# Shifted value tiles of the first batch made by TensorE with a shifted identity in place of a second read from scratch, with a newly searched order

**The chip, the cores and the metric.** One core of one Trainium2 chip. The metric is the device time of one execution in microseconds (us); a lower time is better. Of several executions the median is quoted with the lowest and highest. The runs of this study fell on several chips, and the same kernel took about 230 us on one and about 239.5 us on two others; so kernels are compared only with the kernel before on the same chip, by their ratio.

## The reference

Block-sparse attention over 4 batches, 8 heads, 768 positions and 64 values a head, followed by a gated feed-forward layer. The mask lets a block of 32 queries see its neighbours, the first and the last block, and three random blocks.

```python
def _attn_ref(q, k, v, sampled_blocks):
    ...                                   # scores = q k^T / sqrt(64)
    mask = np.abs(blk_i - blk_j) <= 1     # window
    mask = mask | (blk_i == 0) | (blk_j == 0) | (blk_i == n_blocks - 1) | (blk_j == n_blocks - 1)
    ...                                   # plus three sampled blocks for each block of queries
    return softmax(scores where mask) @ v

def _moe_ref(x, w_in, g_ln, w_sg, b_sg, w_out):
    h = gelu(x @ w_in); u, v = halves of h
    v_s = einsum('ts,bsd->btd', w_sg, layer_norm(v) * g_ln) + b_sg
    return x + (u * v_s) @ w_out
```

## The kernel before

The kernel is one list of named operations. Each has an engine, the keys that it reads and writes, and a function that issues the instructions. Every engine runs its own operations strictly in the order of the list; the waits are derived from the keys.

```python
SEQ = """ ... regsP0 w_in0 ... ga0.3
vg0.0 kp0.5 ga0.5 ... va0.0 va0.1 ... vs0 ga0.4 vg0.1 ... vgc0 ... exG0.1 pvG0.0:4 pvW0.0 ga0.1 pvR0.0 ... """
```

V of a batch is written to a scratch area in memory and read back in several layouts.

```python
for n in range(2):
    def vg_(e, n=n):                                   # rows 0-31 and 736-767 of V
        return e.dma_start(vj[64 * n:64 * n + 64, 0, :, :].rearrange("p h e -> p (h e)"),
                           bass.AP(sc.tensor, sc.offset, [[736 * 520, 2], [520, 32], [1, 520]]))
    op("SP", f"vg{b}.{n}", vg_, r=[("scr", bp)], w=[("vjg", n)] + [("vjp", p_) for p_ in range(4)], ..., nbytes=66560)

def vgc(x): ...                                        # compact copy of both halves: VG
op(("DVE", "ACT"), f"vgc{b}", vgc, r=["VGz", ("vjg", 0), ("vjg", 1)] + ..., w=[("VG", n) for n in range(4)], ...)
op("SP", f"vs{b}", lambda e: e.dma_start(VS[...], sc[64:704, :]...), r=[("scr", bp)], w=["VS"], ..., nbytes=665600)
op("SP", f"va{b}.1", lambda e: e.dma_start(VA[:, 1:5, ...], sc[128:640, :]...), ..., nbytes=532480)
...                                                    # va.0 and va.5: the first and the last tile of VA
```

VA holds V in six tiles of 128 rows. VS holds the same rows 64 rows later. VG holds the rows of the first and last block, which every query sees. The attention of a group of queries is three kinds of product into one accumulator: `pvG` with VG, then `pvW` with VA and VS, then `pvR` with the gathered random blocks VR. So VG comes first.

The softmax here doesn't subtract the row's maximum and nothing guards it: scores larger than these inputs give would overflow.

## Time and profile before

| | kernel before |
|---|---|
| time, first three runs | 232.17 us median (229.5 to 235.98) |
| time on the chip of the first experiments | 230.41 us median (229.43 to 232.35, 7 runs) |
| span of the profile shown in the prediction | 240.6 us |
| span of a second profile, taken among the experiments | 227.6 us |

The profile that the prediction reads is of an execution of 242.57 us, well above the median, and so it is no fair partner for the changed kernel. The comparisons below use the second profile, of an execution of 229.72 us. The head of its page: the span, and the busy time of the engines (share of the span, instructions).

```profile
span 227.6 us, 8125 instructions
PE 199.9 (88%) x3282; PEld 159.9 (70%) x3282; DVE 157.1 (69%) x469; ACT 166.9 (73%) x254; POOL 110.3 (48%) x207
```

The busy times by stretches of the same profile (columns as the prediction explains them):

```profile
22.70:36.00 13.30, 7.40 (x228) 5.92 (x230) 5.50 (x27) 8.88 (x14) 11.75 (x26) 0.50 1.10 245
36.00:57.40 21.40, 18.08 (x458) 14.25 (x455) 12.35 (x42) 16.97 (x23) 11.78 (x20) 0.90 1.00 208
57.40:227.60 170.20, 166.42 (x2555) 134.77 (x2551) 130.68 (x370) 126.26 (x195) 77.51 (x139) 1.00 0.66 159
```

TensorE (the first pair) is idle for 5.9 + 3.3 us in the first two stretches. The timelines of SyncE's queue, VectorE and TensorE show the chain that the change attacks (start, duration, then the idle time before and what ended it):

```profile
20.40 0.70 SPq L572 DMA_DIRECT2D vj<-scr  x1
22.05 0.52 SPq L582 DMA_DIRECT2D VS<-scr  x1
25.10 0.55 SPq L572 DMA_DIRECT2D vj<-scr  x1
32.52 0.47 DVE L332 COPY VG<-vj 64x260 bf16<-64x260 bf16 x2 [3.70 <-DMA vj<-scr]
33.13 0.59 PE L335 MATMUL PS<-VG,PG 128*128 128x130 bf16 x4 [3.38 <-DVE VG L332]
```

The second half of VG is issued at 25.10 us, the copy runs at 32.52 us, and the first value product starts at 33.13 us after a wait of 3.38 us.

### The profile page before, as it was taken

To read this page: it belongs to the slowest core of one execution; us is meant where nothing else is said; L and a number is where in the kernel's file an instruction comes from. 1 tells how busy PE (TensorE), PEld (TensorE's weight loads), DVE (VectorE), ACT (ScalarE), POOL (GpSimd) and SP (SyncE) were. 2 spreads that over 40 slices of the span, in tenths; PEclk is the share of its full clock that TensorE was granted. 3 is DMA by queue.
4 is the path that set the end of the run, shared out by engine and by line. 5 is a ranking of instruction groups with operands and counts; after the bars stand their busy time and mean duration, and the time that the engine had idled before them with its cause. 6 is when DMAs were issued, how large, how long until landed. Compare 5 with 4: busy or idle time off the path is not lost.

```text
span 240.6 us, 8125 instructions
## 1 busy us (share of the span) xinstructions
PE 206.9 (86%) x3282; PEld 164.1 (68%) x3282; DVE 157.0 (65%) x469; ACT 166.9 (69%) x254; POOL 109.3 (45%) x207
## 2 busy tenths in 40 slices
PE   5064538879999989999699999799999999999994
PEld 2053426558887678887488687678886778789672
DVE  2453323645796978894648967648668957577694
ACT  3497926868698946898479666578999677976100
POOL 8215984544384856911547373803472752012000
PEclk9999999988999999999979999999999999999999
DMA  6999999759997795985977975690588123311007
GB/s 191 341 368 282 268 198 228 141 116 235 277 212 178 217 241 75 214 130 183 219 192 169 275 150 185 153 179 9 138 258 208 36 54 119 111 46 44 3 0 262
DMA packets 34457, 41.51 MB, mean 173 GB/s; under 512 B 4804, under 2 KB 27620, under 8 KB 34420
## 3 DMA queue, kind: packets, MB, share of 16 engines
q0 software_dynamic: 14208, 16.20, 35.7%
q1 hardware_dynamic: 20212, 24.80, 34.0%
q8 instruction: 26, 0.43, 0.7%
q14 instruction: 11, 0.09, 0.1%
HBM read 39.72 MB, written 9.55 MB: 205 GB/s over the span
## 4 chain that ended last, share of the span: by engine, by line
PE 78%; ACT 9%; DMA 3%; SPq 3%; issue 3%; another core or an unknown queue 2%; DVE 1%
PE PS L335 68%; PE PS L848 5%; PE PS L521 4%; DMA x_tok<-in_q_dram 3%; ACT PW L707 2%; SPq L480 2%; ACT PR L750 1%; ACT QD L331 1%; ACT PG L724 1%; PE PS L659 1%; ACT w_sgT L331 1%; ACT qn L331 1%; ACT L724 1%; ACT bsg L331 1%
## 5 line engine op out<-in xcount | busy, mean ns | idle before, releaser
L616 POOL DMA_INDIRECT VR<-scr,IDX x44 | 43.2, 982 | 20.5 <-issue 8.3
L637 POOL COPY KR<-KT 128x128 bf16 x88 | 26.0, 328 | 24.7 <-PE PS L335 19.9
L335 PE MATMUL PS<-w_sgT,vh 128*128 128x384 bf16 x192 | 33.5, 326 | 0.0
L633 DVE COPY KR<-KT 128x128 bf16 x176 | 28.3, 226 | 4.1 <-PE PS L335 3.2
L335 PE MATMUL PS<-w_in,xg 128*128 128x512 f32 x96 | 28.3, 422 | 3.1 <-ACT xg L331 2.2
L335 PE MATMUL PS<-w_out,xg 128*128 128x512 f32 x96 | 26.3, 409 | 0.0
L335 PE MATMUL PS<-xg,w_in 128*128 128x384 f32 x128 | 26.2, 351 | 0.0
L916 DVE SCALAR_TENSOR_TENSOR gt<-PS,gcol,bsg 128x384 f32<-128x384 f32 x32 | 19.3, 613 | 10.1 <-PE PS L335 9.3
L335 PEld LDWEIGHTS PS<-w_sgT,vh 128*128 128x128 bf16 x192 | 17.9, 98 | 11.0 <-issue 0.4
L750 ACT ACTIVATE PR<-PS 96x1024 bf16<-96x1024 f32 (+1 forms) x23 | 21.7, 962 | 5.0 <-PE PS L335 2.8
L335 PEld LDWEIGHTS PS<-xg,w_in 128*128 128x128 f32 x128 | 23.1, 194 | 1.7 <-ACT QD L331 0.3
L707 ACT ACTIVATE PW<-PS,b_odd 128x512 bf16<-128x512 f32 (+1 forms) x24 | 15.5, 652 | 9.2 <-PE PS L335 9.2
L335 PEld LDWEIGHTS PS<-w_in,xg 128*128 128x128 f32 x96 | 17.2, 194 | 6.9 <-ACT xg L331 2.7
L874 POOL TENSOR_TENSOR lnt<-lnmv,lnc 128x2 f32<-128x2 f32 x12 | 2.4, 200 | 42.5 <-DVE lnmv L870 41.8
L707 ACT ACTIVATE PW<-PS,b_even 128x512 bf16<-128x512 f32 (+1 forms) x24 | 15.6, 651 | 8.0 <-remote 4.4
L934 DVE TENSOR_TENSOR x_tok<-PS,x_tok 128x512 f32<-128x512 f32 x24 | 16.3, 685 | 5.7 <-PE PS L335 5.5
L869 DVE BATCH_NORM_STATS2 lnst<-vg 128x6 f32<-128x512 f32 x24 | 16.1, 682 | 5.6 <-ACT vg L867 5.6
L829 DVE RECIPROCAL rden<-PS 128x8 f32<-128x8 f32 x24 | 4.9, 205 | 22.7 <-PE PS L335 20.6
L335 PEld LDWEIGHTS PS<-w_out,xg 128*128 128x128 f32 x96 | 17.1, 189 | 3.3
L331 ACT ACTIVATE QD<-PS 64x768 bf16<-64x768 bf16 x18 | 14.4, 803 | 6.3 <-PE PS L335 4.5
L724 ACT ACTIVATE PG<-PS 128x512 bf16<-128x512 f32 x24 | 13.9, 598 | 6.4 <-PE PS L335 6.3
L335 PE MATMUL PS<-VA,PW 128*64 128x65 bf16 x384 | 17.5, 199 | 0.1
(122 smaller groups left out, 438.4 us busy)
## 6 DMA issues: line engine op xcount, KB each, us to landing
out_dram<-x_tok SPq DMA_DIRECT2D x20, 256.0 KB, 2.3
VR<-scr SPq DMA_DIRECT2D x114, 32.5 KB
scr<-vj SPq DMA_DIRECT2D x4, 780.0 KB, 4.7
VS<-scr SPq DMA_DIRECT2D x4, 650.0 KB
kn<-in_v_dram POOLq DMA_DIRECT2D x6, 384.0 KB
kn<-in_k_dram POOLq DMA_DIRECT2D x6, 384.0 KB
qn<-in_q_dram POOLq DMA_DIRECT2D x6, 384.0 KB, 7.3
VA<-scr SPq DMA_DIRECT2D x4, 520.0 KB
```

Source lines behind the costliest of these rows:

```text
L331: return x.activation(o_, i_, ACT.Copy)
L335: return pe.matmul(o, l, r, start=start, stop=True, skip_group_check=True)
L616: return g.indirect_dma_start(out=vt[0:96, :, :].rearrange("p h e -> p (h e)"), out_offset=None, in_=scr[bp][:, :], in_offset=bass.Indirec ...
L633: ins = x.tensor_copy(KR[:, :, rg, 32 * j:32 * j + 32], KT[:, :, bass.ds(vals["DVE", j, i], 32)])
L637: op("POOL", f"kp{b}.{i}", lambda x, i=i, rg=rg: x.tensor_copy(KR[:, :, rg, 64:96], KT[:, :, bass.ds(vals["POOL", 2, i], 32)]), r=kk + [(" ...
L707: return a.activation(o, i_, ACT.Exp, bias=bias[:, 0:1], scale=SCALE)
L724: op("ACT", f"exG{b}.{tau}", aft=ga, fn=lambda a: a.activation(PG[pg_][:, :], PS[:, uG.slot * 512:uG.slot * 512 + 512], ACT.Exp, scale=SCALE),
L750: return a.activation(PR[pr_][0:96, 0:n], PS[0:96, uR.slot * 512:uR.slot * 512 + n], ACT.Exp, scale=SCALE)
L848: ins = pe.transpose(PS[:, cc:cc + P], x_tok[bp][:, tau, kt * P:kt * P + P], ident_f[:, :])
L869: op("DVE", f"bs{b}.{tau}", lambda x: x.bn_stats(lnst[:, vr, :], vg[vr][:, :]), r=[("vg", vr)], w=[("lnst", vr)], dur=0.6, prio=pr - 300)
L916: op("DVE", f"g1{b}.{c}{dt}", lambda x: x.scalar_tensor_tensor(gt[gr][:, :], PS[:, u.slot * 512:u.slot * 512 + 384], gcol[:, dt:dt + 1], b ...
L934: op("DVE", f"res{b}.{tau}", lambda x: x.tensor_tensor(x_tok[bp][:, tau, :], PS[:, u.slot * 512:u.slot * 512 + 512], x_tok[bp][:, tau, :], ...
```

## The change

Its intent: in batch 0, where transfers bound the kernel, drop the 650 KB read of VS and let TensorE make the five tiles. A product of VA's tile with an identity that is shifted by 64 columns moves rows by 64 partitions; two such products into one accumulator give one tile of VS for half the heads. The shifted identity lives in the buffer of the later tile `bsg`, so the profile shows the shift products as `PS<-VA,bsg`. With it comes a wholly new list, found by a search in which landings were assumed late. One more line of the diff is not shown: an operation on GpSimd now also waits for a zeroing or padding operation (names in `ze` and `pa`) that stands just before it there.

```diff
+    op(("DVE", "POOL"), "i3z", lambda x: x.memset(I3, 0.0), w=["I3"], ...)
+    op("POOL", "i3", lambda g: g.affine_select(I3, I3, compare_op=ALU.not_equal, fill=1.0, base=64, ...), ...)
...
-        op("SP", f"vs{b}", ... VS <- sc[64:704] ..., w=["VS"], nbytes=665600)
+        if b == 0:
+            for t in range(5):
+                def shf(pe, t=t, u=u):
+                    for c in range(2):
+                        for n in range(2):
+                            ins = mm(pe, PS[:, o:o + 260], I3[:, 128 - 128 * c:256 - 128 * c],
+                                     VA[:, t + c, 4 * n:4 * n + 4, :]..., c == 0)
+                ...  op("PE", f"shf{t}", shf, r=["I3", ("VA", t), ("VA", t + 1)], ...)
+                     op(("DVE", "ACT"), f"she{t}", copy accumulator -> VS[:, t], ...)
+        else:
+            op("SP", f"vs{b}", ... as before, w=[("VS", t) for t in range(5)])
...
-SEQ = ... the old list ...
+SEQ = ... padv:P csq0.1 ... vg0.0 va0.1 csk0.3 ... qkG0.1:0 shf1:6 ga0.1 ... va0.0 shf3:2 ... shf0:0 ... she0 vg0.1 ... vgc0 pvG0.0:6 ...
+      ... gV1.5 bs1.5 ... vg2.0 vg2.1 ba1.5 ... qkQ2.1:0 vgc2:A gU1.02 nv1.3:A nv1.2:A nv1.4:A ...
```

## The prediction

> **What bounds the kernel now.** I read the page first, then the busy time of each engine by stretches, then TensorE's waits in the start, then who waited for the scratch reads, and last the issues of SyncE in order of time. The stretches were chosen by hand at the places where TensorE changes from waiting to working.
>
> Busy time in each stretch; the first pair of numbers is the stretch and its length, then busy time (instructions) of PE, PEld, DVE, ACT and POOL, the granted clock, the DMA share and the rate:
>
> ```profile
> 0.00:22.70 22.70, 8.88 (x55) 5.59 (x55) 8.46 (x33) 14.91 (x22) 9.47 (x24) 1.00 0.90 296
> 22.70:36.00 13.30, 6.97 (x204) 5.49 (x204) 4.75 (x24) 7.75 (x14) 11.74 (x26) 1.00 1.08 237
> 36.00:57.40 21.40, 17.66 (x423) 13.82 (x421) 10.21 (x40) 15.18 (x21) 11.46 (x20) 0.92 0.82 175
> 57.40:237.00 179.60, 172.97 (x2606) 139.23 (x2603) 133.13 (x373) 129.04 (x199) 76.61 (x139) 0.99 0.64 151
> ```
>
> From 57.4 to 237 us TensorE is busy 172.97 of 179.60 us (96%): that part is TensorE's own work, and the change touches it only through a new order. In the first 57.4 us TensorE idles 13.8 + 6.3 + 3.7 = 23.9 us, and there the DMA share is 0.8 to 1.1, that is, all 16 queues have work almost without a gap. So batch 0 is bound by transfers, batches 1 to 3 by TensorE.
>
> What TensorE waited for between 22 and 50 us (total, times, longest):
>
> ```profile
> PE PS L335 <- DVE VG L332: 2.9, 1, 2.9
> PE PS L335 <- ACT w_sgT L331: 2.6, 1, 2.6
> ...
> PE PS L335 <- ACT PW L707: 1.2, 1, 1.2
> PE PS L335 <- DVE KR L633: 1.1, 1, 1.1
> ```
>
> The largest is the first product with V (at 32.84 us), which waits for the compact tile VG. The reads behind VG, and who waited for them:
>
> ```profile
> L572 SPq DMA_DIRECT2D vj<-scr x8: 537/553/692, 20.3 to 177.6; - x8
> ...
>   DVE VG L332: 3.5, 1
> ```
>
> So VG in its turn waits for a read of scratch. SyncE's issues show why that read is late:
>
> ```profile
> 20.27 0.69 SPq L572 DMA_DIRECT2D vj<-scr  x1
> 21.02 0.38 SPq L580 DMA_DIRECT2D VA<-scr  x1
> 21.43 0.43 SPq L584 DMA_DIRECT2D VA<-scr  x1
> 21.91 0.52 SPq L582 DMA_DIRECT2D VS<-scr  x1
> 22.65 1.37 SPq L611 DMA_DIRECT2D VR<-scr  x3
> 24.90 0.56 SPq L572 DMA_DIRECT2D vj<-scr  x1
> ```
>
> The second half of VG (24.90) stands behind VA, behind the 650 KB of VS, and behind a gather. VectorE copies it at 32.3 us, some 7 us after its issue. VS is the shifted value tile: the same rows as VA, 64 rows later, read a second time.
>
> **What the Trainium skill says.** "DMA: Bandwidth & Descriptors", section Issuing engines are not separate DMA queues: transfers started by different engines run on the same 16 DMA engines and interleave. The trace agrees: the reads of scratch share 20 to 32 us with w_in and the gathers of GpSimd, at a share of 1.09. [...]"TensorE: Matmul & The Clock Gate", section Back-to-back issue gap, gives N/2.4 + 2.5 ns warm and N/1.2 ns cold, and section LDWEIGHTS columns/1.2. The trace agrees on loads (98 ns for 128 bf16 columns) and on two speeds: the 16 value products of a group start about 27 ns apart at 33.5 us and 17 ns apart at 47 us.
>
> **The change, part by part.** (1) Removed: one read of 650 KB, in batch 0 only, of 41.51 MB in all. Between vg's first half (20.27) and VG's copy (32.3) the SyncE queue moved about 65 + 98 + 520 + 650 + 98 + 65 KB = 1.5 MB in some 11.3 us, 0.13 MB/us, because it shares with GpSimd's queue. At that rate 650 KB are worth 0.65/0.13 = 5.0 us; at the whole stretch's 280 GB/s they are worth only 2.3 us. So VG, and the first value product with it, can come 2.3 to 5 us earlier: 28 to 30.5 us in place of 32.84.
>
> (2) Added on TensorE: 5 tiles of 4 products, 260 columns each. By the page's formula, an estimate, 111 ns warm or 217 ns cold each, beside loads of 98 ns: 0.45 to 0.9 us a tile, 2.2 to 4.4 us in all. Three of the five stand before the first value product, in idle TensorE time (6.3 us of it between 22.7 and 36). Two (shf2, shf4) stand among later work, where TensorE is 83% busy: about 1 us of real cost.
>
> (3) Added evictions: 128x520 from the accumulator to the tile. A like ACT eviction (PG, 128x512 to bf16) took 598 ns, a like DVE one (xg, 128x512) 679 ns; two on ACT and three on DVE give 1.2 + 2.1 = 3.3 us. Both engines are under 60% busy from 22.7 to 36 us. Only the one before the first value product (she0, 0.7 us) could be on the path, and it overlaps the wait for VG.
>
> (4) Added set-up: a memset and a select for the shifted identity, under 1 us (the like ones took 0.21 and 0.29 us), in GpSimd's idle 8.4 us of the start. Six warming products at the start go (2.7 us of TensorE, in its idle time).
>
> (5) The order. V is loaded first, so the write to scratch no longer waits for the tenth load. Before it was issued at 15.53 us and scratch could be read at 20.27. At one load per 1.06 us (landings at 13.58, 14.64 and 15.69), V's four loads among the first five land at about 10.3, the copies end near 12, and the write goes out there. It stands behind the q loads already queued, though, so I give it 1 us. One k load now follows the write: 4.7 + 0.8 MB still must pass before the first scores, which stay at about 22.5 us (22.77 before). w_in can start earlier on GpSimd, at 11 to 12 in place of 16.64 us, which takes bandwidth from q but returns it to V.
>
> (6) The rest of the list is a new search result with no other change in work. TensorE's idle time from 57.4 to 237 us is 6.6 us, and of it a new list may win or lose a couple.
>
> Sum: the first value product 3 to 5 us earlier, less 1 us of TensorE for two shifts, less what a later wait gives back. The next ones are gathers: the first gather product also has waits for instructions in it (0.50 and 0.52 us at 35 us), and ACT stood 4.4 us before 35.88 with a releaser that the profile doesn't know. If a third comes back, 2 us remain in the first stage; for the search with late landings I add 1.5 us. The profiled run took 242.57 us against a median of 232.17, so the profile shows more waiting than the timed runs have, which is why I keep to the lower end. 232.2 - 2.0 - 1.5 is 228.7, I say 228.5.
>
> **The rivals.** First, the read was hidden anyway: the gathers for the same group (SyncE's nine issues from 25.66 us, 5.1 us long) may end the wait instead. For: pvR0.0 comes directly after. Against: those gathers stand in the same queue behind VS and move forward with it. Time: 231 to 233. Second, a wait takes the place of the removed one: the shift products stand in TensorE's list ahead of the scores of the other tiles, so a late VA holds up scores that had not needed VA. For: VA is 520 KB and read after the later write. Against: it is now second in the queue. Time: 232 to 235. Third, the load order loses: a k load behind the scratch write and w_in earlier could move the first scores to 24 or 25 us. Time: about 231. Fourth, the searched order is robust: fewer late landings stop TensorE, so idle from 36 us on falls by half (5 us) as well. For: the three runs before spread from 229.5 to 235.98, as a kernel at the mercy of its landings would. Time: 223 to 226.
>
> **Range and chances.** The bounds: the work on TensorE after 22.7 us is 6.97 + 17.66 + 172.97 = 197.6 us; with 1 to 2 us of shifts, a start at 22.5, 3.6 us of tail and 2 us outside the span, the floor is about 227 in the profile's own speeds, somewhat less with a warmer clock. So gains beyond 9 us are nearly out; 223 is my lower end. Upper end 233.5, where a new wait eats all. Faster by over 2% means under 227.5: 0.40; within 2%: 0.52; slower: 0.08.
>
> **What would show it.** Right: no VS read in batch 0; the first product with VG at 28 to 30.5 us; TensorE's wait for VG below 1 us; 20 products with the shifted identity of 0.45 to 0.9 us a tile; TensorE idle of 22.7 to 57.4 us down from 10 to 6 or 7 us; first scores at 22 to 23.5 us. Wrong: a new long wait of TensorE for VA in front of shf1, first scores after 24 us, a first value product still after 32 us, or more TensorE idle after 57 us than 6.6 us. The number is wrong too if the new list changes batches 1 to 3 by more than 3 us, which I can't read from the list.

## The result and the profile after

The changed kernel took 239.72 us median (238.25 to 240.25, 4 runs) against 231.75 us (229.5 to 235.98, 4 runs): a ratio of 1.0367 with a 95% interval of 1.027 to 1.0464. It is slower by over 2%. A ratio here is the mean time of one kernel's fast runs over the mean of the other's fast runs of the same rounds, so it is not quite the ratio of the medians. Two further controls on two chips gave 1.0303 and 1.0323.

The head of the page of the changed kernel (execution of 238.25 us):

```profile
span 236.4 us, 8156 instructions
PE 203.8 (86%) x3296; PEld 164.2 (69%) x3296; DVE 159.7 (68%) x474; ACT 165.7 (70%) x252; POOL 110.8 (47%) x209
```

Of the 8.8 us between the spans (236.4 against 227.6) TensorE's busy time accounts for 203.8 - 199.9 = 3.9 us and its idle time for the other 4.9 us. The two profiles may be of different chips; the two controls below, on one chip, differ in span by 9.6 us (237.2 against 227.6). By stretches:

```profile
22.70:36.00 13.30, 9.23 (x207) 6.72 (x202) 6.01 (x31) 8.61 (x14) 10.52 (x24) 0.96 1.04 195
36.00:57.40 21.40, 17.99 (x454) 13.99 (x452) 11.14 (x46) 16.78 (x24) 12.11 (x23) 0.87 0.88 178
57.40:236.40 179.00, 170.28 (x2587) 138.01 (x2584) 132.32 (x368) 126.54 (x198) 74.89 (x138) 0.98 0.64 153
```

From 22.7 to 57.4 us TensorE's idle time is 4.1 + 3.4 = 7.5 us against 9.2 us before: it did fall. But after 57.4 us it is 8.7 us against 3.8 us. (The clock of 0.96 says little here: the trace's first clock record is at 31.54 us.) The list of TensorE's waits (total, times, longest), without the 11.9 us before its very first product:

```profile
...
PE PS L338 <- ACT vh L919: 4.6, 2, 4.2
PE PS L338 <- issue: 3.3, 3, 2.2
PE PS L338 <- DMA VA<-scr: 2.7, 1, 2.7
...
PE PS L338 <- DVE VG L335: 0.8, 1, 0.8
```

Three things stand here. The wait for VG fell from 3.4 to 0.8 us; a new wait for VA of 2.7 us stands in its place; and there is a wait of 4.2 us for `vh`, the gate's input, that the kernel before did not have. (The 2.2 us called `issue` are a pause inside the fourth tile's shift products, up to 40.61 us, for which the profile names no cause; the second profile has 1.84 us there.) The timelines of SyncE's queue and of TensorE in batch 0:

```profile
18.56 0.70 SPq L579 DMA_DIRECT2D vj<-scr  x1
24.06 0.56 SPq L579 DMA_DIRECT2D vj<-scr  x1
26.69 1.91 PE L338 MATMUL PS<-VA,bsg 128*128 128x260 bf16 x8 [2.71 <-DMA VA<-scr]
28.83 1.07 PE L338 MATMUL PS<-VA,bsg 128*128 128x260 bf16 x4
32.50 0.41 PE L338 MATMUL PS<-VG,PG 128*128 128x130 bf16 x4 [0.82 <-DVE VG L335]
```

The first half of VG is issued 1.8 us earlier than before (18.56 against 20.40), VS is gone, and still the first product with VG starts at 32.50 us, only 0.6 us earlier than before. The idle time in which it used to wait now holds twelve shift products (eight in 1.91 us and four in 1.07 us) and a wait for VA ahead of them. The first two tiles took 0.87 us each (from 26.69 us to the next product at 28.43 us).

The `vh` wait is found where batch 1's feed-forward layer meets batch 2's attention. SyncE's queue, ScalarE and TensorE between 110 and 130 us:

```profile
110.02 6.28 SPq L579 DMA_DIRECT2D vj<-scr  x2
121.36 0.85 ACT L334 ACTIVATE VG<-vj 64x260 bf16<-64x260 bf16 x2 [4.35 <-DMA vj<-scr]
125.03 4.02 PE L338 MATMUL PS<-w_sgT,vh 128*128 128x384 bf16 x12 [4.16 <-ACT vh L919]
```

The new list puts the compact copy of VG of batch 2 on ScalarE, ahead of three normalisations (`nv1.3`, `nv1.2`, `nv1.4`) that make `vh` for batch 1. The copy waits 4.35 us for the two halves, everything behind it on ScalarE waits with it, and TensorE stands 4.16 us. The chain that ended last shows why the read took so long (start, length):

```profile
110.02 5.76 DMA vj<-scr
115.79 5.54 DMA vj<-scr
```

The two halves do not overlap. Each has the keys `vjp` among its writes, so the second is ordered behind the landing of the first, although they write different rows. The same holds in batch 0: the issues are at 18.56 and 24.06 us in the timeline above, and the first half's last data landed at 24.04 us. In the prediction's list of issues, too, the second half follows the first by 4.6 us (24.90 us, and the first half landed at 24.89 us); I had read that as standing behind other reads.

The stall costs more than its 4.16 us. Busy times in the five microseconds after it, the changed kernel:

```profile
125.00:130.00 5.00, 4.97 (x29) 2.46 (x30) 2.70 (x7) 3.74 (x6) 0.64 (x1) 0.50 0.51 150
```

After the stall the granted clock is 0.50, and the twelve gate products take 4.02 us. Where no stall stands ahead of them, the same twelve take 2.12 us (a run below). The Trainium skill, "TensorE: Matmul & The Clock Gate", section What's actually happening, says that the array falls to half its clock after about 3.4 us of idleness and needs as long to come back; this trace agrees with the halving, after 4.16 us of waiting.

### The profile page after: what moved, and what is told of

The parts are those of the page before. It is cut to its first block, busy times and chain, and to the rows that moved or that the text cites.

```text
span 236.4 us, 8156 instructions
## 1 busy us (share of the span) xinstructions
PE 203.8 (86%) x3296; PEld 164.2 (69%) x3296; DVE 159.7 (68%) x474; ACT 165.7 (70%) x252; POOL 110.8 (47%) x209
## 4 chain that ended last, share of the span: by engine, by line
PE 60%; ACT 11%; DMA 8%; issue 2%; SPq 2%; POOL 0%; DVE 0%; ACTq 0%
PE PS L338 53%; DMA vj<-scr 5%; PE PS L880 4%; DMA w_out<-in_moe_w_out_dram 3%; SPq L643 2%; PE PS L528 2%; ACT vh L919 2%; ACT QD L334 2%; ACT vg L899 1%; ACT uT L933 1%; ACT L899 1%; ACT KT L334 1%; PE PS L691 1%; ACT PR L782 1%; SPq L972 1%
## 5 line engine op out<-in xcount | busy, mean ns | idle before, releaser
L338 PE MATMUL PS<-w_sgT,vh 128*128 128x384 bf16 x192 | 36.1, 338 | 4.6 <-ACT vh L919 4.6
L669 POOL COPY KR<-KT 128x128 bf16 x88 | 25.0, 316 | 30.4 <-PE PS L338 23.7
L338 PE MATMUL PS<-w_in,xg 128*128 128x512 f32 x96 | 26.6, 409 | 0.0
L338 PE MATMUL PS<-xg,w_in 128*128 128x384 f32 x128 | 23.9, 338 | 0.0
L951 DVE TENSOR_TENSOR xg<-gt,uT 128x384 fp32r<-128x384 f32 x32 | 17.8, 566 | 0.5
L899 ACT ACTIVATE vg<-PS 128x512 f32<-128x512 f32 x24 | 14.1, 596 | 4.8 <-PE PS L338 4.5
L865 DVE TENSOR_TENSOR x_tok<-PS,rden 128x512 f32<-128x512 f32 x24 | 16.4, 688 | 0.6
## 6 DMA issues: line engine op xcount, KB each, us to landing
VR<-scr SPq DMA_DIRECT2D x114, 32.5 KB, 2.9
```

The lines of the kernel that those rows point to most:

```text
L338: return pe.matmul(o, l, r, start=start, stop=True, skip_group_check=True)
L669: op("POOL", f"kp{b}.{i}", lambda x, i=i, rg=rg: x.tensor_copy(KR[:, :, rg, 64:96], KT[:, :, bass.ds(vals["POOL", 2, i], 32)]), r=kk + [(" ...
L865: return x.tensor_tensor(x_tok[bp][:, tau, :].rearrange("p (a h d) -> p a h d", a=2, h=4), ap(PS, 0, P, uO.slot * 512, [[512, 2], [65, 4], ...
L899: op("ACT", f"gV{b}.{tau}", lambda a: a.activation(vg[vr][:, :], PS[:, u.slot * 512:u.slot * 512 + 512], ACT.Gelu_apprx_tanh), r=[("vp", b ...
L951: op("DVE", f"g2{b}.{c}{dt}", lambda x: x.tensor_tensor(xg[2 + c][:, dt, :], gt[gr][:, :], uT[c][:, dt, :], ALU.mult), r=[("gt", gr), ("uT ...
```

## The experiments

Sixteen runs were made, all with correct results, in four jobs. The first two jobs ran on one chip (kernel before: 230.41 and 230.34 us median), the third on a second chip (239.51 us) and the fourth on a third (239.68 us). Some records are missing from the traces, more of them on the two slower chips. One execution of the kernel before in the fourth job took 482.26 us; it counts as slow and is in no ratio.

| run | kernel | median us | ratio to before | 95% interval |
|---|---|---|---|---|
| b_again | before | 229.78 | 0.998 | 0.9929 to 1.0032 |
| a_again | changed | 240.07 | 1.0303 | 1.0198 to 1.0409 |
| e1_order_only | changed, VS read, no shifts | 243.18 | none | none |
| e3_vg_early | changed, VG of batch 2 read earlier | 240.66 | 1.0424 | 1.0358 to 1.049 |
| e4a_vg_free_old | changed, halves of VG independent | 237.24 | 1.0267 | 1.0211 to 1.0322 |
| e4b_vg_free_new | before, halves of VG independent | 229.59 | 0.9943 | 0.9893 to 0.9993 |
| e2_shift_old_order | before's list with shifts | 232.37 | 1.0054 | 0.9981 to 1.0126 |
| e5_shift_vg_free | the same, halves of VG independent | 231.35 | 0.9975 | 0.9918 to 1.0032 |
| e6_vgc2_late | changed, VG copy of batch 2 later | 243.52 | 1.0197 | 1.0113 to 1.0281 |
| e7_vg16_old | before, VG read in 32-row pieces | 239.46 | 0.9967 | 0.9868 to 1.0066 |
| e8_vg16_new | changed, VG read in 32-row pieces | 243.22 | 1.0188 | 1.0101 to 1.0274 |
| e9_half_shift | changed, shifts on half the array | 247.24 | 1.0344 | 1.0246 to 1.0441 |
| a_third | changed | 249.72 | 1.0323 | 1.0251 to 1.0395 |
| e10_all_vg_new | changed, all repairs of VG | 243.3 | 1.0094 | 1.0029 to 1.0159 |
| e11_all_vg_old | before, VG repairs | 239.57 | 0.9955 | 0.9897 to 1.0012 |
| e12_all_vg_shift | before's list with shifts, VG repairs | 242.34 | 1.0106 | 1.0062 to 1.015 |

**The theory and its rivals.** Theory: the loss comes from VG, which is late for reasons other than VS, first in batch 0 and then, through ScalarE, in batch 2. Rival one: the shift products themselves cost the time on TensorE. Rival two: the new list loses in many small places.

### Controls: both kernels again

> The kernel before, unchanged, for a profile of a typical run: the one shown before was 242.57 us where the others were 229.5 to 235.98. Both theories expect 230 to 236 us and a ratio of 1.00. If the profile is of a run near 231 us, its TensorE waits from 22 to 57 us should be 4 to 8 us fewer than in the first profile (there 10.1 us of idle).

> The changed kernel, unchanged, on the same chip: 238 to 240 us, ratio 1.03 to 1.04 if the loss is the program's; 1.00 to 1.01 if it was the chip of that job. VG of batch 2 at 121 us again if the late copy of VG is the program's doing.

The times came out as in the first measurement (two of the four executions of the changed kernel count as slow). One expectation was missed: from 22.7 to 57.4 us the typical profile of the kernel before has 9.2 us of TensorE's idle time against 10.1 us in the first profile, not 4 to 8 us less. In the second profile of the changed kernel the shift products, grouped by form (busy us, mean ns, idle before), read:

```profile
L338 PE MATMUL PS<-VA,bsg 128*128 128x260 bf16 x20 | 5.1, 413 | 5.7 <-DMA VA<-scr 3.8 <-issue 1.8
```

5.1 us busy for 20 products, and 5.7 us of idle time ahead of them, 3.8 us of it for VA. I also read from the traces of the two controls when each stage's last instruction ended (no view of the profile; all records of these instructions are there):

| stage | before, us | changed, us | difference |
|---|---|---|---|
| attention of batch 0 ends | 60.1 | 64.1 | 4.0 |
| normalisations of batch 0 end | 72.9 | 77.2 | 4.3 |
| attention of batch 1 ends | 106.7 | 106.8 | 0.1 |
| layer statistics of batch 1 end | 115.9 | 118.8 | 2.9 |
| normalisations of batch 1 end | 119.9 | 126.8 | 6.9 |
| first gate product of batch 1 evicted | 122.8 | 129.2 | 6.4 |
| first finished group of batch 2's attention | 135.4 | 143.0 | 7.6 |
| first gate product of batch 2 evicted | 169.0 | 179.2 | 10.2 |
| first gate product of batch 3 evicted | 211.9 | 221.6 | 9.7 |

The third row shows that the new list does other work earlier or later, so not every difference is a loss. A loss of 4 us stands after batch 0, one of about 6.5 us where batch 1 gives way to batch 2, and one of 10 us from 179 us on.

### The list alone

```diff
- ... shf0..shf4, she0..she4 (changed kernel)
+ va0.1 vs0 csk0.3 ...      # VS of batch 0 read from scratch again, the rest of the new list kept
```

> The changed kernel's order, with the five shift products and their five evictions taken out and the second read of scratch put back behind the read of VA. Theory A (the searched order of batches 1 to 3 loses the time): stays at 236 to 240 us. Theory B (the shift products, which stand ahead of scores and wait for VA, lose it): back to 230 to 233 us.

Measured 243.18 us (239.15 to 243.66), with no ratio, since three of the four executions, the profiled one among them, count as slow. The fast one took 239.15 us; beside the changed kernel of the same job (fast ones 239.11 and 235.78 us) it is not faster. So taking the shifts out of the new list does not bring the time back: the list loses it with or without the shifts. How much the shifts save in this list stays open. (In the profile, of a slow execution and so only a hint, VG is copied at 34.43 us with VS read, against 31.45 us in the control without.)

### VG of batch 2 read earlier

```diff
- ... vg2.0 vg2.1 ba1.5 ...
+ ... sc2 vg2.0 vg2.1 ...   # right behind the write to scratch
```

> The changed kernel with the two reads for VG of batch 2 issued straight behind that batch's write to scratch, instead of behind three gathers and an output on SyncE. Theory A1 (ACT waits 4.4 us for VG in front of the activations that TensorE needs, TensorE idles 4.2 us at 121 to 125 us and its clock falls): 4 to 6 us faster than the changed kernel, 233 to 236 us, and no wait of TensorE over 1 us there. Rival (that wait only moves to the next resource): under 1.5 us gained.

Measured 1.0424: no gain. ScalarE no longer waits for VG, but SyncE, which runs in order, now stands for the write to scratch and for the first half of VG ahead of the gathers of batch 1, and TensorE waits for a gather:

```profile
PE PS L337 <- DMA VR<-scr: 6.3, 1, 6.3
```

A wait was only moved. The experiment cannot tell the theories apart.

### The false dependency removed

```diff
-  w=[("vjg", n)] + [("vjp", p_) for p_ in range(4)]
+  w=[("vjg", n)] + ([("vjp", p_) for p_ in range(4)] if n == 0 else [])
```

The second half is still behind the first in SyncE's list and behind all readers of the tile, so nothing races. **The two labels are swapped by my mistake:** the run named "old" is the changed kernel, the run named "new" is the kernel before. Each expectation below therefore belongs to the other run.

> The kernel before, with one false dependency taken out: the second half of VG's read no longer waits on SyncE for the first half's landing (the two write different partitions). Theory: the two reads of VG run one after the other only because of that dependency, and that, not the VS read ahead of them in the queue, made VG late. Then TensorE's wait for VG in batch 0 (3.4 us) falls under 1.5 us and the time by 1.5 to 4 us, to 226 to 229 us. Rival (VG is late because the queues are full): VG still comes after 31 us and the time stays within 1 us of 230.

> The changed kernel with the same false dependency taken out. Theory: SyncE, which issues in order, stands still for 5 to 6 us in front of each second half; in the searched order gathers and reads that TensorE needs stand behind it. Then the 4 us wait of TensorE at 123 to 127 us goes and batch 0 gains too: 232 to 236 us. Rival (the order's loss lies in batch 0's shifts): only 0 to 2 us gained, 238 to 240 us.

The changed kernel with the edit took 1.0267 (control in the job before: 1.0303), the kernel before with it 0.9943. The edit is worth about half a per cent to each at most and is not the loss. For the kernel before, the rival came true: the second half went out at 23.83 us in place of 25.10, and still VG was copied at 32.73 us (32.52 before), and TensorE waited longer for it, not under 1.5 us:

```profile
33.46 0.59 PE L335 MATMUL PS<-VG,PG 128*128 128x130 bf16 x4 [4.12 <-DVE VG L332]
```

So while VS is read, the order of the halves is not what makes VG late in the old list. In the changed kernel the copy came 0.65 us earlier than in its control (30.80 against 31.45 us), which is within the spread between runs.

### The shifts in the old list

```diff
 # the kernel before's list, the changed kernel's code
- vs0
+ va0.5                                  # moved forward to VS's place
- exG0.1 pvG0.0:4
+ exG0.1 shf0:4 shf1:0 she0:D she1:A pvG0.0:4
+ ... shf2:0 she2:D ... shf3:4 she3:D ... shf4:4 she4:D
```

> The kernel before's own order, with the second read taken out and the five shift products and evictions put in by hand where two banks were free, all else as it was. Theory A (the searched order loses the 9 us, the shifts are nearly neutral): 229 to 232 us. Theory B (shifts cost their 4.4 us of TensorE in full, since batch 0 from 36 us on is already full on TensorE): 232 to 235 us. Prediction's own step (the read removed is worth 2.3 to 5 us of earlier VG): 227 to 229 us.

> The run with shifts in the old order, and the false dependency taken out as well. If the removed read and the freed VG help one another, 2 us under the faster of the two alone; if the first product then waits for VA and its shift instead of VG, no better than the freed VG alone.

Measured 1.0054 and, with the halves of VG independent, 0.9975, against 0.9943 for the same repair with VS read. So the change's own idea, without its list, is neutral: +0.5% and +0.3% (0.9975/0.9943), with no difference that the intervals can tell from zero. TensorE's timeline of the first of them:

```profile
30.77 1.92 PE L337 MATMUL PS<-VA,bsg 128*128 128x260 bf16 x8
33.78 0.41 PE L337 MATMUL PS<-VG,PG 128*128 128x130 bf16 x4 [1.09 <-DVE VS L334]
```

VG was copied at 30.91 us, 1.6 us earlier than with VS read (32.52). The first product with it started 0.65 us later (33.78 against 33.13), because it now waits for the eviction of the shift products, whose accumulator I gave to it. The gain was there and the shifts took it. With the halves independent the pair came out otherwise: without VS, VG was copied 2.85 us earlier (29.88 against 32.73 us) and the first product started 0.76 us earlier (32.70 against 33.46 us), after a wait of 1.76 us for the same eviction.

### The two parts of VG's lateness, one at a time

Each half of VG is one read whose outermost source dimension has two elements. In the trace of the kernel before, its semaphore rises in three steps: the first half's at 21.5, 25.07 and 25.08 us, the second's at 26.08, 32.38 and 32.5 us. That of VS, 650 KB issued at 22.05 us, rose from 27.5 to 29.75 us (13 of its steps are recorded). So the second half, issued 3 us after VS, landed 2.75 us after it: it did come in behind VS, but that alone does not say how much of its 7.4 us VS cost. The Trainium skill, "DMA: Bandwidth & Descriptors", section Why a DMA increments its semaphore by 16 and not by 1, explains such steps: the number of queues is the largest number up to 16 that divides the outermost dimension on both sides, here two, and the count of the unused ones is added at once. The trace agrees. Cutting each read in two, of 32 rows each, makes sixteen of it:

```diff
-  e.dma_start(vj[64*n:64*n+64, ...], bass.AP(..., [[736*520, 2], [520, 32], [1, 520]]))
+  [e.dma_start(vj[64*n+32*i:64*n+32*i+32, ...], sc[736*i:736*i+32, :]) for i in range(2)]
```

The other edit leaves the read and moves the copy behind the evictions and the normalisations:

```diff
- vgc2:A gU1.02 nv1.3:A ... gU1.00 gU1.03
+        gU1.02 nv1.3:A ... gU1.00 gU1.03 vgc2:A
```

> The changed kernel with one copy moved: the copy of VG of batch 2 stands on ACT behind the six activations that batch 1's spatial product needs, instead of ahead of them. Theory (half of the loss is ACT standing 4.4 us at 117 to 121 us for VG, in order, in front of those activations): 234 to 237 us, 3 to 5 us under the changed kernel's 240, and TensorE's wait for the activation of vh falls from 3.8 us to under 1. Rival (the wait moves on to the first product with VG, as it did when VG was read earlier): under 1.5 us gained.

> The kernel before, with each half of VG's read cut into two reads of 32 rows. In the traces each half comes with three steps of its semaphore, one at once and two when data land, where the reads of VA come with sixteen: so it runs on two of the 16 queues. Theory (VG is late because it runs on two queues; neither VS ahead of it nor the dependency made it late): VG is copied by 29 us in place of 33.0, TensorE's 3.4 us wait for it goes, 226 to 229 us. Rival (full queues): still after 31 us and within 1 us of 230.

> The changed kernel with the same cut of VG's reads. Theory: SyncE's two waits of 5.8 and 5.5 us at 110 to 121 us shrink to some 2 to 3 us each, VG of batch 2 is there by 116 us, the 4 us stall of TensorE at 123 to 127 us goes, and batch 0 gains 1 to 3 us: 232 to 236 us. Rival (the queues themselves are full there): 238 to 240 us.

Measured: the later copy 1.0197, the cut read in the changed kernel 1.0188, in the kernel before 0.9967. In the kernel before, VG was copied at 30.12 us, and TensorE's wait ahead of the first product with it is shorter and ended by something else:

```profile
30.99 0.59 PE L335 MATMUL PS<-VG,PG 128*128 128x130 bf16 x4 [1.09 <-ACT PW L706]
```

In the changed kernel it was copied at 29.19 us, against 32.02 and 30.89 us in the two runs of this job that left the read as it was. So the two queues were a cause. The expectation of 29 us was missed by 1.1 us, and that of 226 to 229 us in time too: 0.9967 is no clear gain. In the changed kernel, either edit makes TensorE's long wait for `vh` go: the longest is 0.4 us in the first and 0.5 us in the second, in place of 4.2. This job had no control of the changed kernel, so these two ratios are suggestive only; the last job has one.

### Cheaper shifts

```diff
- mm(pe, PS[:, o:o+260], I3[:, 128-128*c:256-128*c], VA[:, t+c, ...], c == 0)
+ mm(pe, PS[z:z+64, o:o+260], ident[a:a+64, a:a+64], VA[a:a+64, t+c, ...], True)   # (a, z) = (64, 0), (0, 64)
```

> The changed kernel with each shift product made on half of the array's rows and columns: 64 rows to 64 columns, no accumulation, the two halves of a tile side by side; the same 20 products. Theory (the shifts cost 0.87 us of TensorE a tile, 4.3 us in all, and are paid in full): if the halves overlap, 0.45 us a tile and 1.5 to 2.5 us gained, 237 to 238.5 us. Rival (shift time is hidden under waits for transfers): within 0.7 us of the changed kernel's 240.

The edit worked as meant; grouped by form:

```profile
L338 PE MATMUL PS<-VA,ident 64*64 64x260 bf16 x20 | 3.0, 421 | 4.1 <-DMA VA<-scr 4.1
```

3.0 us in place of 5.1, and the ratio, 1.0344, is no lower than the three controls of the changed kernel (1.0303 to 1.0367). So the theory that the shifts are paid in full finds no support here. The test is weak, though: its interval (1.0246 to 1.0441) is as wide as the 1.5 to 2.5 us that the theory named, and the job had no control of the changed kernel.

### All of VG's lateness at once, with and without shifts

> The changed kernel once more, unchanged, as the control on the chip of these four runs, since the runs with the later compact copy, with the split reads and with the half-array shifts had no control of the changed kernel on their slower chip. Both theories: ratio to the kernel before 1.027 to 1.045, as twice before; on a chip as slow as the last one perhaps only 1.02 to 1.035.

> The changed kernel with all that can hold VG back taken away at once: the second half no longer waits for the first, each half is two reads of 32 rows, and the compact copy of batch 2 stands behind the eviction of the next products on ScalarE. Theory that the late VG of batch 2 (4.2 us of TensorE) and of batch 0 (0.8 us) is half of the loss: 4 to 6 us less than the control, a ratio to the kernel before of 1.01 to 1.02. Rival, that the order of the list is lost in many small places and the wait only moves to the next name: within 1.5 us of the control, a ratio of 1.03 or more, and TensorE's lost time from batch 1's end to the first gate products of batch 2 stays above 5 us.

> The kernel before with the same two repairs of the read of VG (no wait for the first half, two reads of 32 rows each), with VS still read from scratch: this attacks the wait that the change was meant to attack. If VG was the bound of the first value product, it starts at 28 to 30 us instead of 33, and the ratio is 0.98 to 0.995 (1 to 4 us less). If the gathers behind it then end the wait, or the order has no use for an early VG, 0.995 to 1.0.

> The kernel before's order with the shift products put in by hand and both repairs of VG. If the shifts gain something once VG is out of the way, this is the fastest of all, 0.975 to 0.99. If the shift products' 4 us on TensorE are then no longer hidden in the wait for VG, it is slower than the run with the repairs and VS read: 0.995 to 1.01.

The edits are those above, together (the later copy only in the changed kernel, whose list has the stall). The changed kernel came from 1.0323 to 1.0094: of 3.2 points 2.3 are gone, some 70%, on the same chip, with intervals that don't touch. That is the theory's number and not the rival's. TensorE's timelines, first the control, then the repaired kernel:

```profile
32.49 0.41 PE L338 MATMUL PS<-VG,PG 128*128 128x130 bf16 x4 [0.89 <-issue]
131.08 3.24 PE L338 MATMUL PS<-w_sgT,vh 128*128 128x384 bf16 x12 [3.45 <-ACT vh L919]
```

```profile
30.38 0.64 PE L338 MATMUL PS<-VG,PG 128*128 128x130 bf16 x4
124.71 2.12 PE L338 MATMUL PS<-w_sgT,vh 128*128 128x384 bf16 x12
```

The first product with VG comes 2.1 us earlier. The twelve gate products ahead of which TensorE had stood (batch 1's; the expectation calls them batch 2's) start 6.4 us earlier and take 2.12 us in place of 3.24: they run at full clock. The 2.1 us of batch 0, if they carried over, and the stall of 3.45 us would make 5.6 of the 6.4 us; the other 0.8 us I did not trace. Two of the three repairs act on both batches, so this run does not divide the 2.3 points between batch 0 and the stall.

The old list with both repairs and VS read gave 0.9955, with both repairs and shifts 1.0106. The intervals don't touch: once VG is early, the shifts cost 1.0106/0.9955, or 1.5%. TensorE's timelines, VS read and then shifts:

```profile
30.92 0.59 PE L335 MATMUL PS<-VG,PG 128*128 128x130 bf16 x4 [1.69 <-DVE VG L332]
```

```profile
31.60 0.61 PE L337 MATMUL PS<-VG,PG 128*128 128x130 bf16 x4 [0.43 <-DVE VS L334]
```

Again VG itself is earlier without VS (copied at 28.78 against 30.23 us, by 1.45 us) and the product with it later, by 0.7 us. (The 1.5% rests on the timed runs, not on these two profiles.) All runs of the old list together, as copy of VG / first product with VG in us:

| VG's read | VS read | VS made by shifts |
|---|---|---|
| as it was | 32.52 / 33.13 | 30.91 / 33.78 |
| halves independent | 32.73 / 33.46 | 29.88 / 32.70 |
| 32-row pieces | 30.12 / 30.99 | not run |
| both repairs | 30.23 / 30.92 | 28.78 / 31.60 |

Each line is of one chip; the lower two lines are of the two slower chips. (With VG's read as it was, the copy ran anywhere from 30.89 to 32.02 us in five profiles of the changed kernel.) Read across, VS holds VG back by 1.45 to 2.85 us; read down, the two queues hold it back by some 2.4 us, and the order of the halves by nothing while VS is read and by 1.0 us once it is not. So VS is one cause of the lateness and not the only one. And an early product is worth little: with both repairs and VS read it started 2.2 us earlier than in the typical profile (of another chip), and the time fell by 0.45%, with an interval that includes no gain at all. In both runs of the old list the second alternative of the expectation came true.

The changed kernel with the repairs stands at 1.0094, the old list with shifts and repairs at 1.0106: once VG is out of the way, no difference between the two lists is seen (the intervals overlap), and what remains has the size of the price of the shifts. Rival two loses most of its ground with that; what it keeps is that the list put a copy that may be late where it stops TensorE.

**A version that beats both.** The best ratios are of the kernel before with VG repaired in one way or another: 0.9943, 0.9967 and 0.9955. They agree on about half a per cent, only the first interval excludes 1, and none reaches 2%.

## Why the prediction was wrong

- **VG stands behind VS, "and the first value product with it" (step 1): this step failed at its second half.** VG does stand behind VS: without VS it was copied 1.6, 2.85 and 1.45 us earlier in the old list, at the low end of the 2.3 to 5 us or below. The step missed that VG's read runs on two queues, which cost about as much (some 2.4 us), and in the changed kernel, with VS gone, VG was copied only 0.7 us earlier (31.86 against 32.52 us). What did not follow is the product: it started at 32.50 us in the changed kernel, where VG itself stayed late, and not at 28 to 30.5; in the old list it started from 0.76 us earlier to 0.7 us later, because there the shift products and their evictions became the last thing waited for. Nor is it shown that an early product pays: 2.2 us of it came with a gain of 0.45%, not clear of noise. In the working, 1.5 MB took 12.0 us and not 11.3 (20.27 to 32.3), and in 4.6 us of them the second half had not been issued; the trace has the copy at 32.13 us, not 32.3; and the sum begins with 3 to 5 us where the step had 2.3 to 5.
- **Shift products hidden (step 2): size right, hiding only half right.** A tile took 0.87 us of TensorE while its products stood 0.22 us apart, and the last one, with 0.11 to 0.12 us between products, 0.46 us: the two ends of the 0.45 to 0.9 predicted. While VG is late they stand in its wait. But they stand in TensorE's list ahead of the first value product, and with VG repaired they cost 1.5% in the whole. I had put them at 1 us; 1.5% is 3.6 us of 239.7.
- **Evictions off the path (step 3): wrong in the hand-made list** (the first value product waited 1.09, 1.76 and 0.43 us for one, since I gave it their accumulator); in the changed kernel's first profile no such wait appears.
- **Loads and first scores (step 5): held, and better.** VG's first half went out 1.8 us earlier (1 us predicted) and the first scores came at 22.28 us (22.5 predicted). It bought little: the second half waited for the first to land and went out 1.0 us earlier (24.06 against 25.10 us).
- **The searched list (step 6) was given a gain of 1.5 us: this step failed in sign.** I allowed that it could change batches 1 to 3 by a couple of microseconds, and wrote that the number would be wrong if it were more than 3. The copy of VG of batch 2 stopped ScalarE for 4.35 and TensorE for 4.16 us, and the half clock after it cost 1.9 us more (4.02 against 2.12 us). On one chip, 2.3 of the 3.2 points of the loss went with the repairs of VG. A list searched with late landings had been read as robust; it placed the one copy that depends on the slowest read where lateness costs most.
- **The rivals.** The second, a wait for VA in front of the shift products, came true (2.7 us, 3.8 us in the second profile), but it fills time that VG would have taken. The first, that another wait ends the gain anyway, is nearest to what was seen in batch 0, though it was the shift products and their evictions and not the gathers. The fourth, robustness, is the opposite of what happened.
- **The warning signs** that the prediction named were the right ones: a wait for VA in front of shf1, a first value product after 32 us and more idle time after 57 us all showed. Some signs of being right showed as well (TensorE's wait for VG at 0.8 us, the size of the shift products), so they were no test of the gain. The profile before already held the second half's issue, 4.6 us after the first; I did not ask what ordered the two.

What stays open: the 2.6 us that the stage table adds between 143 and 179 us (7.6 to 10.2) were isolated by no run, and neither were the last 0.8 us of the 6.4 that the repairs gave back, the pause of 2.2 us inside the shift products, or what stood ahead of VG in the changed kernel, where the second half landed 7.8 us after its issue although VS was gone.

## What to carry to other kernels

Before removing a large transfer to make a small one earlier, ask what really ends the small one's wait: what orders it, how many queues it uses, and when the large one landed. A helper that fills an idle wait is free only as long as the wait is there, so repair the wait first and then measure the helper. In a list that each engine runs in order, an operation that depends on the slowest read belongs behind everything that others wait for; here a stall of 4.16 us on TensorE was followed by half its clock for the work after it.

## What the Trainium skill lacked or had wrong

- "DMA: Bandwidth & Descriptors" gives the rule for the number of queues, which these traces confirm, and a bandwidth per engine, but not how late a read on few queues lands when they are loaded: here 65 KB over two queues took 7.4 us from issue to landing while 650 KB over sixteen took 7.7 us, and with all repairs the compact copy in the changed kernel moved from 31.81 to 28.77 us.
- No page that I read speaks of the difference between chips: the same kernel took 230.4 us on one, 239.5 and 239.7 us on two others, so a ratio needs its control on the same chip.
